# Attention and a gated feed-forward on one core: GpSimd's masks and copies kept from the place right behind a DMA issue, and the order's biases made anew

## The chip, the cores and the metric

One core of one Trainium2 chip runs the whole program. Its engines are TensorE (PE: matmuls and transposes), VectorE (DVE), ScalarE (ACT), GpSimd (POOL) and SyncE (SP, which here only issues transfers). The time is in device microseconds. The kernel before took 303.01 us (median of 3 runs, 302.78 to 303.18).

## The reference

Two layers follow each other. The first is attention over 8 batches, 8 heads, 576 positions and 64 dimensions a head, with a causal mask that lets each query see 32 keys: in the first four heads the last 32 positions, in the other four every fourth of the last 128. The second is a feed-forward from 512 to 2048 and back to 512 over all 4608 tokens, with a gate h * sigmoid(beta * h).

```python
rel = pos[:, None] - pos[None, :]
mask_plain = (rel >= 0) & (rel < 32)
mask_dil = (rel >= 0) & (rel < 128) & (rel % 4 == 0)
attn = softmax(where(mask, q @ k.T / 8, -1e9))          # plain for heads 0..3, dil for 4..7
x = (attn @ v)                                          # (tokens, heads * 64) = (4608, 512)
h = x @ w_in                                            # (4608, 2048)
out = (h / (1 + exp(-beta * h))) @ w_out                # (4608, 512), float32
```

## The kernel before

**Feed-forward.** The 4608 tokens are cut into nine tiles of 512. For each tile and each of 16 blocks of 128 hidden columns, four matmuls (line 887) multiply w_in with the transposed activations `xT` into one bank of PSUM; ScalarE takes a tanh (L896), and VectorE forms the gate `g` (L901). Then 16 matmuls for each 128 tokens (L922, in four parts of four; parts three and four need the second half of w_out) give the output, which ScalarE or VectorE scales (L937, L939) and SP stores (L942).

**Attention.** It is worked batch by batch between the matmuls of the feed-forward. Batches 0 to 2 load q and k directly, and TensorE transposes them (L469, L479); batches 3 to 7 cast them to scratch in memory (GpSimd's queue) and read them back through transposing transfers (L460, on SP's queue). Scores are L652 (tail), L683 (dilated), L711 and L747 (plain); ScalarE takes the exponent (L619); from batch 1 on a mask of zeros and ones is multiplied in afterwards (L623, on VectorE or GpSimd), while batch 0 adds its mask by a matmul (L673, L733, L736). Values are L773 (tail), L788 (dilated) and L804 (plain); VectorE divides by the sum (L638, L639). For batches 0 and 1 TensorE transposes the result into `xT` (L826, L841, L856); later ones go through memory and a transposing transfer (L506 to L533). Copies between tiles (`dkt`, `qt`, `vd`, the halo rows of `vp`) are all on line 243, transfers that GpSimd or SP issues on L394.

**Who sets the order.** All instructions are first recorded as operations with their dependences, a due time `vt`, the engines that may do them, and an expected duration. `Plan.run` then walks a model of the machine forward in time: it keeps when each engine is free, which banks of PSUM are held, how many transfers are in flight on a queue (eight at most), and picks for each engine, of the operations that could start within a few tens of ns of the first (`NEAR`), the one that is due first. So both the order on each engine and the choice of engine come out of it. The order is then fixed in the program: each engine runs its list in order, waiting only for semaphores.

Three details matter for the change:

- Operations that read and write SBUF alone are marked `sbuf` (masks, copies, halo rows, and the making of mask_d and mask_n). Of two such ones on VectorE and GpSimd the model lets only one run at a time (`port`).
- `NUDGE` is a table from an operation's number to a bias in ns, which is added to its possible start when operations are compared. It changes which one is chosen, not any duration.
- Where the model sees TensorE free for more than a bound before the next matmul, in the first 80 us, a filler matmul on zeros is put in (L1035).

GpSimd's copy on L1001 (`pace`) waits until a part of an earlier batch's `xT` (or, for batch 3, of `g`) is there; all loads of a later batch stand behind it.

The comparison in which the change puts its new bound reads, before:

```python
if o.sbuf:
    at = {e: max(t, port["DVE" if e == "POOL" else "POOL"]) for e, t in at.items()}
fin = min(at[e] + d for e, d in o.engs)
```

Of the kernel before, what the change touches and what calls it, by code (L numbers as in the profile page):

```python
# [39 lines left out]
class Plan:  # L40
# [3 lines left out]

    CAPS = {"h": 3, "p": 4, "o": 2, "z": 4, "a": 8, "s": 5, "w": 6}
    SWITCH = 95
    NUDGE = {9: -400, 35: 400, 78: -150, 90: 150, 103: -900, 156: -900, 164: -60, 191: -60, 208: 150,
        220: 900, 247: -400, 251: 60, 266: -150, 268: -150, 270: -150, 326: 900, 376: 400,
        397: 900, 420: 900, 432: -900, 490: 900, 525: 150, 545: 60, 554: 900, 562: -60, 571: 60,
        574: 150, 1103: -400, 1113: 400}  # L50
    LAT = {"PE": 210, "ACT": 45, "DVE": 45, "POOL": 60, "SP": 0}
    NEAR = {"PE": 40, "ACT": 60, "DVE": 60, "POOL": 60, "SP": 0}

# [3 lines left out]
    def op(self, engs, fn, deps=(), vt=0.0, acquire=None, group=None, dma=0, lat=None, halves=False, sbuf=False):  # L57
        acquire = acquire if acquire is None or isinstance(acquire, list) else [acquire]
        o = Op(engs, fn, deps, vt, acquire, group or acquire, dma, lat, halves, sbuf)
        o.bias = self.NUDGE.get(len(self.ops), 0)  # L60
        self.ops.append(o)
        return o

    def run(self, filler=None, filler_until=0.0):
        free = {"PE": 1100.0, "ACT": 1300.0, "DVE": 1000.0, "POOL": 1300.0, "SP": 1300.0}
        dma_free = {"POOL": 0.0, "SP": 0.0, "ACT": 0.0}
        lanes = {"POOL": [], "SP": [], "ACT": []}
        bank_free = {b: 0.0 for b in self.banks}
        held = {}
        for o in self.ops:  # L70
            for d in o.deps:
                d.next.append(o)
            o.waits = len(o.deps)
            o.ready = 0.0
        avail = [o for o in self.ops if not o.waits]
        n_left = len(self.ops)
        n_held = {k: 0 for k in self.CAPS}
        ends = []
        halves = False
        port = {"DVE": 0.0, "POOL": 0.0}  # L80

        def release(now):
            for g in list(ends):
                if g.release <= now:
                    ends.remove(g)
                    n_held[g.kind] -= 1

        def bank_at(gs, start):
            kind, more = gs[0].kind, len(gs)
            n = [x.release for x in ends if x.kind == kind and x.release > start]  # L90
            n_open = sum(1 for x in held.values() if x.kind == kind)
            if n_open + more > self.CAPS[kind]:
                return None
            over = n_open + len(n) - self.CAPS[kind] + more
            if over > 0:
                start = sorted(n)[over - 1]
            open_banks = {x.bank for x in held.values()}
            times = sorted(t for b, t in bank_free.items() if b not in open_banks)
            return max(start, times[more - 1]) if len(times) >= more else None

        while n_left:
            best = None
            near = {}
            for o in avail:
                base = o.ready
                at = {e: max([free[e], base] + [t for x, t in o.group.read.items() if x != e]
                             if o.group is not None and e != "PE" else [free[e], base]) for e, d in o.engs}
                if o.sbuf:
                    at = {e: max(t, port["DVE" if e == "POOL" else "POOL"]) for e, t in at.items()}
                fin = min(at[e] + d for e, d in o.engs)  # L110
                for e, d in o.engs:
                    start = at[e]
                    if start + d > fin + 100:
                        continue
                    if o.dma and len(lanes[e]) >= 8:
                        start = max(start, lanes[e][-8])
                    if o.acquire is not None:
                        start = bank_at(o.acquire, start)
                        if start is None:
                            continue  # L120
                    near.setdefault(e, []).append((start, o, d))
            picks = []
            for e, c in near.items():
                first = min(s + o.bias for s, o, _ in c)
                s, o, d = min((x for x in c if x[0] + x[1].bias <= first + self.NEAR[e]), key=lambda x: (x[1].vt, x[0]))
                picks.append((s, o.vt, e, o, d))
            assert picks, "no work can start"
            s, _, e, o, d = min(picks, key=lambda x: (x[0], x[1]))
            if filler is not None and s <= filler_until and free["PE"] + (300 if free["PE"] < COLD else 170) < s:
                now = free["PE"]  # L130
                open_banks = {x.bank for x in held.values()}
                spare = [b for b, t in bank_free.items() if b not in open_banks and t <= now]
                if spare:
                    filler(max(spare, key=lambda b: -bank_free[b]))
                free["PE"] = now + (225 if now < COLD else 115)
                halves = False
                continue
            for g in o.acquire or ():
                open_banks = {x.bank for x in held.values()}
                g.bank = min((b for b, t in bank_free.items() if b not in open_banks and t <= s + 1e-6),  # L140
                             key=lambda b: -bank_free[b])
                held[id(g)] = g
                g.left = len(g.users)
            o.fn(e)
            if e == "PE" and o.halves != halves:
                halves = o.halves
                d += self.SWITCH
            free[e] = s + d
            if o.sbuf:
                port[e] = s + d  # L150
            o.start, o.end = s, s + d + self.LAT[e]
            if o.group is not None and e != "PE":
                o.group.read[e] = o.end
            if o.dma:
                at = max(dma_free[e], s + d + 900)
                other = max(dma_free.values()) - at
                dma_free[e] = at + o.dma + max(0.0, min(o.dma, other))
                o.end = dma_free[e] + (o.lat or 1100)
                lanes[e].append(o.end)
            avail.remove(o)  # L160
            n_left -= 1
            for x in o.next:
                x.waits -= 1
                x.ready = max(x.ready, o.end)
                if not x.waits:
                    avail.append(x)
            for g in list(held.values()):
                if o in g.users:
                    g.left -= 1
                    if not g.left:  # L170
                        del held[id(g)]
                        g.release = max(u.end for u in g.users)
                        bank_free[g.bank] = g.release
                        ends.append(g)
            ends[:] = [g for g in ends if g.release > s - 5000]
        self.end = max(free.values())
# [892 lines left out]
```

## Time and profile before

| what | us |
|---|---|
| median of the runs | 303.01 |
| profiled execution, its own time | 302.73 |
| its span, first to last instruction | 301.0 |
| PE busy | 295.5 |
| DVE / ACT / POOL busy | 187.5 / 172.2 / 83.9 |
| L922 and L887 matmuls, busy | 140.0 and 137.0 |
| filler matmuls (L1035), busy | 11.6 |
| GpSimd's transfers, share of 16 DMA engines | 59.5% |

Times of instructions are from the start of the span. A line of a timeline gives start, duration, engine, source line, operation, output and inputs, shapes, how many equal ones are merged, and in brackets how long the engine was idle before and what ended that. Matmuls overlap each other, and their ends are modelled: their starts tell more than their durations.

### The profile page before, as it was taken

The numbers are of one execution on the slowest core, as the hardware profiler recorded it, in microseconds if no ns is written. First come the engines' busy times: TensorE is split into PE (matmuls) and PEld (weight loads), VectorE is DVE, ScalarE is ACT, GpSimd is POOL, SyncE is SP. The second block draws the span as 40 slices with busy tenths as digits, with TensorE's granted clock in tenths as the row PEclk, the third lists the DMA queues.
The fourth block names the chain that finished last, engine by engine and source line by source line (L and its number), as shares of the span: only waits on it lengthen the run. The fifth ranks groups of instructions, "written<-read, shape, count | busy, mean of one in ns | idle before, by whom it ended". The sixth has DMA issues, their size and how long they took to land.

```text
span 301.0 us, 6071 instructions
## 1 busy us (share of the span) xinstructions
PE 295.5 (98%) x2344; PEld 150.4 (50%) x2344; DVE 187.5 (62%) x424; ACT 172.2 (57%) x311; POOL 83.9 (28%) x121
## 2 busy tenths in 40 slices
PE   8999999999999999999999999999999999999995
PEld 5866546444554445544444544444454444444454
DVE  4769787798857846887677647865772363343300
ACT  3868764867745744667484548454852654554311
POOL 8997324764236006400730074000000000000000
PEclk9999999999999999999999999999999999999999
DMA  8999999899889998999899979993124100100122
GB/s 164 188 210 201 206 178 222 122 133 145 196 188 197 158 199 173 199 158 191 145 172 158 224 146 173 179 211 90 37 74 117 70 1 35 37 35 35 59 82 70
DMA packets 111248, 41.98 MB, mean 139 GB/s; under 512 B 87620, under 2 KB 104596, under 8 KB 111220
## 3 DMA queue, kind: packets, MB, share of 16 engines
q0 software_dynamic: 60336, 18.58, 59.5%
q1 hardware_dynamic: 50740, 22.95, 37.8%
q8 instruction: 18, 0.29, 0.4%
q14 instruction: 10, 0.08, 0.1%
q10 hardware_dynamic: 144, 0.07, 0.1%
HBM read 37.76 MB, written 18.87 MB: 188 GB/s over the span
## 4 chain that ended last, share of the span: by engine, by line
PE 94%; DVE 2%; ACT 1%; POOL 1%; issue 1%; POOLq 0%; ACTq 0%
PE bank L922 41%; PE bank L887 40%; PE bank L804 2%; PE bank L1035 2%; PE bank L683 1%; PE bank L788 1%; PE bank L711 1%; PE bank L469 1%; PE bank L747 1%; PE bank L479 1%; ACT ptd L619 1%; PE bank L773 1%; DVE xdm L639 1%; PE bank L673 1%; DVE ptd L623 1%
## 5 line engine op out<-in xcount | busy, mean ns | idle before, releaser
L922 PE MATMUL bank<-w_out_bf,g 128*128 128x512 bf16 (+2 forms) x608 | 140.0, 368 | 0.0
L901 DVE SCALAR_TENSOR_TENSOR g<-tnh,bank 128x512 bf16<-128x512 bf16 x144 | 97.3, 685 | 68.2 <-ACT tnh L896 67.2
L896 ACT ACTIVATE tnh<-bank,beta_half 128x512 bf16<-128x512 f32 x144 | 97.9, 690 | 70.3 <-PE bank L887 63.8
L887 PE MATMUL bank<-xT,w_in_bf 128*128 128x512 bf16 (+1 forms) x584 | 137.0, 376 | 0.0
L887 PEld LDWEIGHTS <-w_in_bf 128*128 128x128 bf16 x584 | 55.7, 98 | 62.8 <-issue 0.3
L922 PEld LDWEIGHTS <-g 128*128 128x128 bf16 x608 | 54.5, 98 | 55.7
L937 ACT ACTIVATE osb<-bank 128x512 f32<-128x512 f32 (+1 forms) x35 | 20.6, 589 | 31.3 <-PE bank L922 30.7
L619 ACT ACTIVATE pt<-bank 128x384 bf16<-128x384 f32 (+1 forms) x54 | 20.8, 467 | 6.8 <-PE bank L711 4.3
L619 ACT ACTIVATE ptd<-bank 128x512 bf16<-128x512 f32 x32 | 16.8, 602 | 6.2 <-PE bank L683 6.2
L639 DVE TENSOR_TENSOR xsp<-bank,rcp 96x384 bf16<-96x384 f32 x32 | 17.7, 554 | 1.3 <-DVE rcp L638 0.2
L623 DVE TENSOR_TENSOR pt<-pt,mask_n 128x384 bf16<-128x384 bf16 (+1 forms) x41 | 14.8, 391 | 5.7 <-ACT pt L619 5.5
L638 DVE RECIPROCAL rcp<-bank 128x4 f32<-128x4 f32 (+2 forms) x72 | 12.8, 178 | 5.5 <-PE bank L804 2.4
L1001 POOL COPY pace<-xT 1x2 bf16<-1x2 bf16 x4 | 0.7, 175 | 51.2 <-DMA xT<-x 51.2
L394 POOL DMA_DIRECT2D vp<-in_v_dram x9 | 14.7, 1632 | 0.4 <-PE bank L469 0.4
L623 DVE TENSOR_TENSOR ptd<-ptd,mask_d 128x512 bf16<-128x512 bf16 x27 | 12.0, 465 | 3.6 <-ACT ptd L619 3.0
L639 DVE TENSOR_TENSOR xdm<-bank,rcp 128x256 bf16<-128x256 f32 x32 | 13.6, 425 | 1.1
L394 POOL DMA_DIRECT2D s<-in_q_dram x10 | 13.5, 1351 | 0.0
L394 POOL DMA_DIRECT2D vt<-in_v_dram x16 | 13.3, 993 | 0.0
L1035 PE MATMUL bank<-zero 128*128 128x256 bf16 x67 | 11.6, 310 | 1.3 <-DVE warm L302 1.1
L394 POOL DMA_DIRECT2D s<-in_k_dram x10 | 11.0, 1100 | 1.4 <-issue 1.1
L804 PEld LDWEIGHTS <-pt 128*128 128x128 bf16 x192 | 8.9, 97 | 4.7
L804 PE MATMUL bank<-vp,pt 128*128 128x65 bf16 x192 | 9.8, 193 | 0.0
(112 smaller groups left out, 172.2 us busy)
## 6 DMA issues: line engine op xcount, KB each, us to landing
out_dram<-osb SPq DMA_DIRECT2D x35, 256.0 KB
s<-in_k_dram POOLq DMA_DIRECT2D x10, 288.0 KB, 7.1
s<-in_q_dram POOLq DMA_DIRECT2D x10, 288.0 KB, 10.0
w_out_bf<-in_moe_w_out_dram POOLq DMA_DIRECT2D x2, 1024.0 KB, 16.5
vp<-in_v_dram POOLq DMA_DIRECT2D x7, 288.0 KB, 17.3
st<-in_q_dram POOLq DMA_DIRECT2D x6, 288.0 KB, 11.1
x<-xsp SPq DMA_DIRECT2D x12, 144.0 KB
st<-in_k_dram POOLq DMA_DIRECT2D x5, 288.0 KB, 13.2
```

The source lines that it names most:

```text
L394: {"POOL": nc.gpsimd, "SP": nc.sync}[queue].dma_start(out=out, in_=in_)
L619: nc.scalar.activation(out=w(), in_=sc(), func=ACT.Exp, scale=SCALE)
L623: E[e].tensor_tensor(out=w(), in0=w(), in1=m(), op=ALU.mult)
L638: nc.vector.reciprocal(out=r, in_=p[..., D])
L639: nc.vector.tensor_tensor(out=dst, in0=p[..., 0:D], in1=r.unsqueeze(len(p.shape) - 1).to_broadcast(list(p.shape[:-1]) + [D]), op=ALU.mult)
L804: nc.tensor.matmul(pv[:, a, h2, :], lhsT=lhs, rhs=vp[kv][:, (2 * x + h2) * NI + 3 * j + a, 0:D + 1], start=True, stop=True)
L887: nc.tensor.matmul(bank(g)[:, a:z], lhsT=w_in_bf[:, kt, fb * P:(fb + 1) * P], rhs=xT[:, kt, xo + a:xo + z], start=(i == 0 and kt == kts[0] ...
L896: nc.scalar.activation(out=th[:, 0:n], in_=bank(g)[:, 0:n], func=ACT.Tanh, scale=beta_half[:, fb:fb + 1])
L901: nc.vector.scalar_tensor_tensor(out=g_t[t % 2][:, fb, c0:c0 + n], in0=th[:, 0:n], scalar=1.0, in1=bank(g)[:, 0:n], op0=ALU.add, op1=ALU.mult)
L922: nc.tensor.matmul(bank(g)[:, lo:hi], lhsT=g_t[t % 2][:, fb, tb * P:(tb + 1) * P], rhs=w_out_bf[:, fb, lo:hi], start=(fb == 0), stop=(fb = ...
L937: nc.scalar.mul(out=ob[:, lo:hi], in_=bank(g)[:, lo:hi], mul=0.5)
L1035: nc.tensor.matmul(BANKS[b][:, 0:256], lhsT=zero[:, 0:P], rhs=zero[:], start=True, stop=True)
```

## The change

In the model, an operation marked `sbuf` may not start on GpSimd until 1200 ns after the end of GpSimd's last DMA issue. The table of biases is a new one: 29 entries before and 29 after, of which only one (operation 1113, 400) is in both. Nothing else in the kernel is edited: operations, shapes, transfers and their sizes stay. Since the order and the engine of a great many operations come out of the model, the lists of all engines differ in many places. Source lines behind the edit move by 5: L887 becomes L892, L922 L927, L1035 L1040.

```diff
     CAPS = {"h": 3, "p": 4, "o": 2, "z": 4, "a": 8, "s": 5, "w": 6}
     SWITCH = 95
-    NUDGE = {9: -400, 35: 400, 78: -150, 90: 150, 103: -900, 156: -900, 164: -60, 191: -60, 208: 150,
-        220: 900, 247: -400, 251: 60, 266: -150, 268: -150, 270: -150, 326: 900, 376: 400,
-        397: 900, 420: 900, 432: -900, 490: 900, 525: 150, 545: 60, 554: 900, 562: -60, 571: 60,
-        574: 150, 1103: -400, 1113: 400}
+    NUDGE = {10: 900, 16: -150, 32: -150, 34: 400, 40: -900, 65: -150, 99: -150, 121: -900, 159: -400,
+        165: -400, 190: -150, 215: 400, 222: -400, 362: 900, 382: -900, 422: -900, 426: -150,
+        443: 900, 537: 400, 553: -400, 656: -150, 836: 400, 838: 400, 881: -150, 914: -60,
+        1113: 400, 1133: -900, 1136: 400, 1158: -400}
...
         halves = False
+        issued = 0.0
         port = {"DVE": 0.0, "POOL": 0.0}
...
+                if o.sbuf and "POOL" in at:
+                    at["POOL"] = max(at["POOL"], issued)
                 if o.sbuf:
                     at = {e: max(t, port["DVE" if e == "POOL" else "POOL"]) for e, t in at.items()}
...
             if o.sbuf:
                 port[e] = s + d
+            elif o.dma and e == "POOL":
+                issued = s + d + 1200
```

## The prediction

> **What bounds the kernel now.** I read the page's engine shares first, then the chain that ended last, then TensorE's timeline, looking only for places where a group starts later than the one before it allows.
>
> The busy shares and the chain, from the page:
>
> ```profile
> PE 295.5 (98%) x2344; PEld 150.4 (50%) x2344; DVE 187.5 (62%) x424; ACT 172.2 (57%) x311; POOL 83.9 (28%) x121
> ...
> PE 94%; DVE 2%; ACT 1%; POOL 1%; issue 1%; POOLq 0%; ACTq 0%
> ...
> L1035 PE MATMUL bank<-zero 128*128 128x256 bf16 x67 | 11.6, 310 | 1.3 <-DVE warm L302 1.1
> ```
>
> TensorE is busy for 98% and is 94% of the chain, so an edit to the order can win only what TensorE wastes: fillers (L1035, matmuls on zeros that keep it busy), stalls, and changes of matmul shape. The other engines are far from full. The granted clock is 9 tenths or more in every slice of the page.
>
> TensorE's own timeline shows the waste:
>
> ```profile
> 1.13 3.81 PE L1035 MATMUL bank<-zero 128*128 128x256 bf16 x17 [1.13 <-DVE warm L302]
> 5.13 1.74 PE L673 MATMUL bank<-add_d,ident_b 128*128 128x512 bf16 x4 [0.19 <-POOL add_d L345]
> ...
> 41.43 0.29 PE L788 MATMUL bank<-vd,ptd 128*128 128x65 bf16 x4
> 41.77 0.38 PE L841 MATMUL bank<-ident_b,xdm 128*128 128x128 bf16 x4
> 42.31 0.49 PE L1035 MATMUL bank<-zero 128*128 128x256 bf16 x3 [0.16 <-DVE xdm L639]
> 42.86 0.38 PE L841 MATMUL bank<-ident_b,xdm 128*128 128x128 bf16 x4
> ...
> 62.93 1.02 PE L887 MATMUL bank<-xT,w_in_bf 128*128 128x512 bf16 x4
> 64.69 0.28 PE L788 MATMUL bank<-vd,ptd 128*128 128x65 bf16 x4 [0.73 <-DVE xdm L639]
> ```
>
> Matmuls overlap, so starts count, not durations. Back to back, a 512-column matmul starts every 0.216 us, a 256-column one every 0.109, a 128-column one every 0.056, a 65-column one every 0.029 (starts of neighbours in the trace). Laid end to end at these intervals, all 2344 matmuls of the trace run without a gap except here:
> - start-up, to 30 us: 0.65 us in pieces of about 0.1;
> - 41.4 to 42.9: L841 could start at 41.55, the fillers 0.22 later, the second L841 another 0.33 later; they start 0.22, 0.32 and 0.22 late, 0.75 us in all. They wait for VectorE's normalisation (L639);
> - 64.69: four L887 from 62.93 end at 63.79, so 0.90 is lost;
> - 91.22: 0.20 lost between L922 and L887.
>
> Some 0.8 us more lies in steps too small to name, and from 91 us on no start is over 0.1 late. The stall at 64.69 is the largest; the timeline of all engines shows how it comes about:
>
> ```profile
> 60.04 0.79 DVE L623 TENSOR_TENSOR ptd<-ptd,mask_d 128x512 bf16<-128x512 bf16 x2
> 60.39 2.18 POOL L394 DMA_DIRECT2D s<-in_q_dram  x1
> 61.39 1.55 DVE L623 TENSOR_TENSOR ptd<-ptd,mask_d 128x512 bf16<-128x512 bf16 x1 [0.55 <-ACT ptd L619]
> 61.51 2.42 POOL L623 TENSOR_TENSOR ptd<-ptd,mask_d 128x512 bf16<-128x512 bf16 x1
> 62.86 1.23 DVE L623 TENSOR_TENSOR ptt<-ptt,mask_t 96x256 bf16<-96x256 bf16 x1
> 64.21 0.42 DVE L639 TENSOR_TENSOR xdm<-bank,rcp 128x256 bf16<-128x256 f32 x1
> ```
>
> A GpSimd mask begins while GpSimd's DMA issue (60.39 to 62.57) is still running and takes 2.42 us. VectorE's masks beside it take 1.55 and 1.23 us, where two like the first had just taken 0.79 together. VectorE reaches L639 some 2 us late, and TensorE waits 0.90 of it. This is the pattern that the change names.
>
> **A rule weighed against the row.** The Trainium skill's page "SBUF — State Buffer", section "Who interferes with whom", says that a VectorE instruction with two SBUF inputs contends with a GpSimd instruction that reads SBUF, whichever comes second being blocked. That names the collision of the two masks, not the DMA issue, and so speaks against a change that keeps GpSimd's masks. By it the new order, with eight masks on GpSimd (seven before), would keep the 0.90: the sum below would be -0.8 instead of -1.7. The trace agrees only in part: GpSimd's other masks, away from a DMA issue, take 0.74 us each (mean of five 288-column ones).
>
> **The change part by part**, with the instruction lists of both built programs beside the trace.
>
> 1. *Fillers.* 67 become 65. At the cold start 17 become 18: +0.21 (3.81 / 17 = 0.22 each). Later 50 become 47: 3 x 0.109 = -0.33. Sum -0.1.
> 2. *Shape changes.* Between 64-row matmuls (L479, L683, L711, L747, L826) and full ones the order changes 58 times before, 56 after. Each adds about 0.1: four L922 take 0.86 us in the chain, 0.97 beside such a group. -0.2.
> 3. *The mask at 61.51.* In this stage all four ptd masks now go to VectorE (two, one normalisation, two); GpSimd does copies only. Cost: one more VectorE mask at 0.42, against 1.13 and 0.95 saved on the two stretched ones. TensorE asks for the results with about 0.5 us to spare when I set VectorE's and ScalarE's rows end to end. -0.9, between 0 (the stretch has another cause) and -0.9.
> 4. *The stall at 41.4.* VectorE's four normalisations (0.55 each) had stood too close to L841. Now two g operations and eight L887 lie between, four of the eight pt masks go to GpSimd (4 x 0.74, from about 38.2), and L841 is asked for about 0.5 us after its input. -0.75, between 0 and -0.75.
> 5. *The 0.20 at 91.2* has no releaser that I can name: -0.1, between 0 and -0.2.
> 6. *GpSimd at the start.* ident_f (0.10 and 0.19 us, 0.36 with gaps) moves ahead of ident_b, so add_d ends at 5.45 instead of 5.08. The first L673 slips 0.36, of which part 1's extra cold filler (0.21) is a share: +0.15. mask_t moves behind the weight loads and six input loads; its reader on VectorE is moved to about 18 us and it ends near 16.5, so 0.
> 7. *Loads.* Up to w_out the GpSimd queue keeps its order, and its transfers land one behind the other (w_in's three parts at 15.98, 18.52, 24.03; first w_out at 35.42, second at 42.10), though issued long before. Two w_in issues come 1.1 us earlier, the first w_out issue 1.2 later: no landing moves, 0. But TensorE, now ahead, asks for the w_out halves at about 35.5 and 42.2: +0.1, between 0 and +0.6. For batch 2 the vp load goes behind the others; read at about 68, landing by 54, so 0.
> 8. *Start-up.* VectorE's and ScalarE's evacuations in the new order, set end to end by hand, make TensorE wait 0.3 for the first scores (L683), 0.2 for the second halo copy, 0.2 to 0.3 for transposes: the 0.65 of before in other places. +0.1, between -0.3 and +0.6.
> 9. *SP's queue.* The crossbar of the next batch's q now stands ahead of batch 2's xsp stores. Its cast is issued one place earlier (before, vp took 5.7 us ahead of it: 67.44 to 73.19 landing), so batch 2's transposed x lands no later than the 87.25 of before; first read at about 88.4: 0.
>
> Sum: -0.1 - 0.2 - 0.9 - 0.75 - 0.1 + 0.15 + 0.1 + 0.1 = -1.7 us. The profiled execution took 302.73 (span 301.0 and 1.73 around it): 301.0 after. The runs' median is 303.01, 0.28 above it; so I say **301.3 us**.
>
> **Rivals.**
> - *The order runs nearly as laid out*: 300.3 to 302.2 by the ends of parts 3 to 8. For it: the intervals account for TensorE's whole time but the stalls named, and these are gone from the order as I lay it out. Against it: the walk is by hand over 60 us. 61%.
> - *The rule does nothing on the chip, stalls return elsewhere.* mask_d still stands directly behind a DMA issue in the list, and no wait is added; GpSimd runs it at once. Then only parts 1 and 2 stay, with one or two of the old stalls back: 303.0 - 0.3 = 302.7, to 302.0 with half of parts 3 to 5. 20%, of which 10% within 0.2%, 10% still faster.
> - *Slower: transposed x comes late.* Two pt masks of batch 5 stand on GpSimd behind the next batch's casts, and these behind the copy that waits for batch 4's transposed x (L1006). That landed at 144.10 before; casts take 7.5 us (54.9 to 62.6), so the masks could start at 151.7, and TensorE needs them from about 155. The first L887 of that tile asks at 143.8 or so. From there each us that the landing is later is a us of TensorE, and the slower side begins where 1.7 + 0.6 are eaten, at a landing of 146.1: 147 gives 301.3 + 3.2 = 304.5. Against it: the loop starts about 1 us earlier (the first such copy at 54 rather than 54.78) and in my walk lands near 139. 13%.
> - *Better than laid out*, start-up and w_out cost nothing and drifts of 0.1 vanish: 299.8 to 300.3. 6%.
>
> **Numbers.** 0.2% (0.6 us) is about what a measurement of this kernel tells from no change. Faster: 61 + 10 + 6, 0.77; same 0.10; slower 0.13. Range 300.2 to 302.9: it leaves out the slower case and part of the best one. The likeliest case alone: 300.3 to 302.2.
>
> **What would show it.** After: 65 fillers; no GpSimd mask over 1.3 us; VectorE masks of 512 columns at 0.4 to 0.5 all through 55 to 65 us; no TensorE gap of 0.7 near 64; L841 not late near 42; TensorE's last matmul at 296.0 instead of 297.7. Wrong if TensorE shows gaps over 0.5 us with DMA as releaser at 35, 42, 88 or 144, or if the start-up loses over 1.3 us.

## The result and the profile after

| | before | after |
|---|---|---|
| median of 20 runs, us | 302.92 | 302.35 |
| lowest to highest, us | 302.67 to 304.32 | 301.13 to 303.21 |
| profiled execution, its own time | 302.73 | 302.39 |
| its span | 301.0 | 300.7 |
| PE / DVE / POOL busy | 295.5 / 187.5 / 83.9 | 294.7 / 183.2 / 90.5 |
| TensorE's last matmul starts at | 297.72 | 297.39 |

The ratio of after to before is 0.9974, with a 95% interval from 0.9963 to 0.9986. The kernel got faster, but by 0.57 us by the medians and 0.8 by the ratio, where 1.7 were forecast, and its runs spread over 2.1 us. Source lines of the changed kernel are those of before plus 5.

The engine shares and the chain, from the page of after:

```profile
PE 294.7 (98%) x2342; PEld 150.2 (50%) x2342; DVE 183.2 (61%) x415; ACT 171.3 (57%) x311; POOL 90.5 (30%) x130
...
PE 83%; DMA 9%; POOL 2%; SPq 2%; issue 1%; DVE 1%; ACT 0%; POOLq 0%
PE bank L892 36%; PE bank L927 35%; DMA vp<-in_v_dram 6%; PE bank L1040 2%; DMA xT<-x 2%; PE bank L809 1%; PE bank L793 1%; PE bank L688 1%; SPq L465 1%; DMA x<-xsp 1%; PE bank L716 1%; PE bank L484 1%; PE bank L474 1%; PE bank L752 1%; POOL s L399 1%
```

TensorE is as full as before, yet its share of the chain fell from 94% to 83%. In its place stands one transfer, `vp<-in_v_dram`, with 6% (18 us), and a little GpSimd and SyncE. The chain now leaves TensorE somewhere and goes through the memory loop.

First, the stalls that the prediction named. TensorE's timeline of after, at the places of the old stalls at 41.8 and 64.7:

```profile
40.46 1.89 PE L892 MATMUL bank<-xT,w_in_bf 128*128 128x512 bf16 x8
42.18 0.39 PE L846 MATMUL bank<-ident_b,xdm 128*128 128x128 bf16 x4
42.40 1.03 PE L927 MATMUL bank<-w_out_bf,g 128*128 128x512 bf16 x4
43.27 0.39 PE L846 MATMUL bank<-ident_b,xdm 128*128 128x128 bf16 x4
...
61.49 1.03 PE L892 MATMUL bank<-xT,w_in_bf 128*128 128x512 bf16 x4
62.36 0.28 PE L793 MATMUL bank<-vd,ptd 128*128 128x65 bf16 x4
62.48 0.41 PE L778 MATMUL bank<-vt,ptt 96*128 96x65 bf16 x8
```

Eight 512-column matmuls from 40.46 end at 42.18 (8 x 0.216), where L846 starts; four from 61.49 end at 62.36, where the last dilated value starts. Neither loses anything. VectorE shows why, all four masks at its usual speed:

```profile
57.72 0.75 DVE L628 TENSOR_TENSOR ptd<-ptd,mask_d 128x512 bf16<-128x512 bf16 x2
...
59.42 0.75 DVE L628 TENSOR_TENSOR ptd<-ptd,mask_d 128x512 bf16<-128x512 bf16 x2
...
61.12 0.42 DVE L644 TENSOR_TENSOR xdm<-bank,rcp 128x256 bf16<-128x256 f32 x1
```

Then the new stall. TensorE, VectorE and GpSimd of after, around batch 4's dilated values:

```profile
110.43 0.29 PE L793 MATMUL bank<-vd,ptd 128*128 128x65 bf16 x4
110.56 1.03 PE L927 MATMUL bank<-w_out_bf,g 128*128 128x512 bf16 x4
112.86 0.30 PE L793 MATMUL bank<-vd,ptd 128*128 128x65 bf16 x4 [1.28 <-DVE ptd L628]
...
109.09 0.43 DVE L628 TENSOR_TENSOR ptd<-ptd,mask_d 128x512 bf16<-128x512 bf16 x1 [2.98 <-ACT ptd L624]
111.86 0.48 DVE L248 COPY vp<-vp 32x1280 bf16<-32x1280 bf16 x1 [2.35 <-DMA vp<-in_v_dram]
112.38 1.10 DVE L628 TENSOR_TENSOR ptd<-ptd,mask_d 128x512 bf16<-128x512 bf16 x3
...
87.80 0.18 POOL L1006 COPY pace<-xT 1x2 bf16<-1x2 bf16 x1 [7.50 <-DMA xT<-x]
...
93.65 2.23 POOL L399 DMA_DIRECT2D vp<-in_v_dram  x1
```

Read it from the bottom. GpSimd's `pace` waits 7.50 us for batch 2's transposed x and lets batch 4's loads go; the last is vp, issued at 93.65 and landed at 111.84. VectorE, whose list has the halo copy of this vp ahead of three masks, waits for it with nothing else to do. TensorE could have started its second group at 111.42 (four L927 behind 110.56) and starts at 112.86: 1.44 us late.

The same wait stood in the profile of before, in VectorE's row, without a price:

```profile
111.49 0.48 DVE L243 COPY vp<-vp 32x1280 bf16<-32x1280 bf16 x1 [2.66 <-DMA vp<-in_v_dram]
112.00 1.62 DVE L623 TENSOR_TENSOR ptd<-ptd,mask_d 128x512 bf16<-128x512 bf16 x4
...
113.08 0.29 PE L788 MATMUL bank<-vd,ptd 128*128 128x65 bf16 x4
...
114.06 0.53 PE L788 MATMUL bank<-vd,ptd 128*128 128x65 bf16 x12
```

There vp had landed at 111.46, and TensorE asked for its first dilated value only at 113.08, after the mask: hidden, with about 0.6 us to spare. In after TensorE is there 2.65 us sooner (110.43 for 113.08), of which 0.86 is the order (four feed-forward matmuls fewer lie before it: 352 for 356) and 1.79 is real lead. The landing is 0.38 later, not sooner. In this profile the forecast of 1.7 us was met at 110 us (with a little luck: 0.21 us of the lead is there at the first feed-forward matmul already, where single profiles differ by more); by 113 us most of it was given back. 1.79 less 1.44 is 0.35, and the last matmul is 0.33 earlier.

### The profile page after: what moved, and what is told of

Same layout as the page of the kernel before. It is cut to its first block, busy times and chain, and to the rows that moved or that the text cites. A ratio compares the mean times of both kernels' runs of the same rounds, so it can differ in the third digit from the quotient of the medians.

```text
span 300.7 us, 6078 instructions
## 1 busy us (share of the span) xinstructions
PE 294.7 (98%) x2342; PEld 150.2 (50%) x2342; DVE 183.2 (61%) x415; ACT 171.3 (57%) x311; POOL 90.5 (30%) x130
## 4 chain that ended last, share of the span: by engine, by line
PE 83%; DMA 9%; POOL 2%; SPq 2%; issue 1%; DVE 1%; ACT 0%; POOLq 0%
PE bank L892 36%; PE bank L927 35%; DMA vp<-in_v_dram 6%; PE bank L1040 2%; DMA xT<-x 2%; PE bank L809 1%; PE bank L793 1%; PE bank L688 1%; SPq L465 1%; DMA x<-xsp 1%; PE bank L716 1%; PE bank L484 1%; PE bank L474 1%; PE bank L752 1%; POOL s L399 1%
## 5 line engine op out<-in xcount | busy, mean ns | idle before, releaser
L927 PE MATMUL bank<-w_out_bf,g 128*128 128x512 bf16 (+2 forms) x608 | 140.2, 368 | 0.0
L892 PE MATMUL bank<-xT,w_in_bf 128*128 128x512 bf16 (+1 forms) x584 | 137.6, 376 | 0.0
L892 PEld LDWEIGHTS <-w_in_bf 128*128 128x128 bf16 x584 | 55.4, 98 | 61.5
L927 PEld LDWEIGHTS <-g 128*128 128x128 bf16 x608 | 55.0, 98 | 56.2
L628 DVE TENSOR_TENSOR pt<-pt,mask_n 128x384 bf16<-128x384 bf16 (+1 forms) x39 | 13.0, 349 | 7.0 <-ACT pt L624 6.5
L643 DVE RECIPROCAL rcp<-bank 96x6 f32<-96x6 f32 (+2 forms) x72 | 12.9, 179 | 6.8 <-PE bank L809 3.4
L628 DVE TENSOR_TENSOR ptd<-ptd,mask_d 128x512 bf16<-128x512 bf16 x27 | 11.0, 423 | 5.8 <-ACT ptd L624 5.0
L1040 PE MATMUL bank<-zero 128*128 128x256 bf16 x65 | 11.0, 314 | 1.1 <-DVE warm L307 1.1
L944 DVE TENSOR_SCALAR osb<-bank 128x512 f32<-128x512 f32 (+2 forms) x4 | 2.1, 525 | 14.5 <-PE bank L927 14.5
```

Source lines behind the costliest of these rows:

```text
L628: E[e].tensor_tensor(out=w(), in0=w(), in1=m(), op=ALU.mult)
L643: nc.vector.reciprocal(out=r, in_=p[..., D])
L892: nc.tensor.matmul(bank(g)[:, a:z], lhsT=w_in_bf[:, kt, fb * P:(fb + 1) * P], rhs=xT[:, kt, xo + a:xo + z], start=(i == 0 and kt == kts[0] ...
L927: nc.tensor.matmul(bank(g)[:, lo:hi], lhsT=g_t[t % 2][:, fb, tb * P:(tb + 1) * P], rhs=w_out_bf[:, fb, lo:hi], start=(fb == 0), stop=(fb = ...
L1040: nc.tensor.matmul(BANKS[b][:, 0:256], lhsT=zero[:, 0:P], rhs=zero[:], start=True, stop=True)
```

## Experiments

All times are medians, set beside runs of the kernel before on the same chip (302.77 to 303.15 there).

| kernel | us | lowest to highest | ratio to before, 95% |
|---|---|---|---|
| after, once more | 302.08 | 301.18 to 303.86 | 0.9957 to 0.9992 |
| after, batch 4's halo copy on GpSimd | 302.20 | 301.72 to 302.37 | 0.9965 to 0.9985 |
| before, one mask moved to VectorE | 302.10 | 301.67 to 302.72 | 0.9963 to 0.9986 |
| before, that mask ahead of two issues | 302.38 | one run | |
| the new bound with the old biases | 308.12 | 306.89 to 309.11 | 1.0145 to 1.0191 |
| the new biases without the bound | 305.17 | 304.77 to 306.01 | 1.0058 to 1.0090 |
| after, batch 4's loads released earlier | 301.53 | 301.35 to 302.75 | 0.9943 to 0.9974 |
| before, batch 4's loads released earlier | 302.93 | 302.70 to 303.46 | 0.9986 to 1.0003 |
| after, both edits of batch 4 | 301.72 | 301.52 to 301.84 | 0.9942 to 0.9966 |
| after, loads of batches 4 to 7 released earlier | 303.53 | 301.43 to 307.46 | 0.9973 to 1.0034 |
| after, eight more matmuls at 92 us | 302.30 | 302.20 to 303.14 | 0.9963 to 0.9989 |
| the same with batch 4's loads earlier | 302.35 | 302.11 to 303.03 | 0.9962 to 0.9984 |

### What a GpSimd mask behind an issue costs

The kernel before, with the one mask that stood there given to VectorE:

```diff
-                    E[e].tensor_tensor(out=w(), in0=w(), in1=m(), op=ALU.mult)
+                    E["DVE" if b == 2 and key[0] in (2, 3) else e].tensor_tensor(out=w(), in0=w(), in1=m(), op=ALU.mult)
```

> The kernel before with one instruction moved: the batch-2 ptd mask that GpSimd does at 61.5 us is done by VectorE, at its place in the program. If the stretched masks cause the stall of 0.90 us at 64.7 in full, VectorE's 512-column masks take 0.4 to 0.5 each there, the stall is under 0.1, and TensorE is 0.9 earlier at 70 us. Theory A then has 0.3 of it taken back at 113, where VectorE's wait for batch 4's vp load leaves about 0.65 of room: -0.6 us, 302.3. Without such a wall: -0.9, 302.0. If the stretch has another cause, the stall stays and the time is 302.9.

302.10 us: 0.67 less than before on the same chip. The 0.89 us at 64.69 is gone, the stall at 41.8 stays. Moving one instruction of the old order is worth about as much as the whole change. TensorE and VectorE of that kernel, at the old stall and where a new one opened:

```profile
62.89 1.03 PE L887 MATMUL bank<-xT,w_in_bf 128*128 128x512 bf16 x4
63.76 0.28 PE L788 MATMUL bank<-vd,ptd 128*128 128x65 bf16 x4
...
169.14 0.48 DVE L243 COPY vp<-vp 32x1280 bf16<-32x1280 bf16 x1 [2.02 <-DMA vp<-in_v_dram]
...
170.14 0.29 PE L788 MATMUL bank<-vd,ptd 128*128 128x65 bf16 x4 [0.29 <-DVE ptd L623]
```

The wait that the expectation placed at 113 us did not come there: in this profile vp landed at 110.30, 1.2 us sooner than in before. It came two batches later, at the halo copy of batch 6, where TensorE starts 0.46 us late. By the starts, TensorE is 1.1 us ahead of before at 91 us (the 0.20 at 91.22 is gone here too) and 0.67 at the end: a second kernel that gives a gain back to a load of vp.

The kernel before, with the mask left on GpSimd but the last two of the eight issues (vp and q's cast) put behind it:

```diff
+            lambda e: held_back.append(lambda: dma(queue, *args)) if hold else dma(queue, *args), ...
...
+                    if b == 2 and key[0] in (2, 3) and e == "POOL":
+                        for late in held_back:
+                            late()
```

> The kernel before with GpSimd's last two issues of batch 3's loads (vp, and the cast of q) put behind the batch-2 ptd mask instead of ahead of it, so that the mask runs with the DMA issue done but with VectorE's masks still beside it. If the running DMA issue stretches it: GpSimd's mask takes 1.2 to 1.4 us and VectorE's beside it under 0.6 each. If two masks on the two engines stretch each other: still over 2 us, and VectorE's third mask over 1 us. Time not the question (the two loads start 1.5 to 2.5 us later).

GpSimd and VectorE of that kernel:

```profile
58.27 1.89 POOL L394 DMA_DIRECT2D vt<-in_v_dram  x2
61.40 1.15 POOL L625 TENSOR_TENSOR ptd<-ptd,mask_d 128x512 bf16<-128x512 bf16 x1 [1.24 <-ACT ptd L621]
62.50 1.23 POOL L394 DMA_DIRECT2D vp<-in_v_dram  x1
...
61.77 1.06 DVE L625 TENSOR_TENSOR ptd<-ptd,mask_d 128x512 bf16<-128x512 bf16 x1 [0.55 <-ACT ptd L621]
62.75 0.28 DVE L625 TENSOR_TENSOR ptt<-ptt,mask_t 96x256 bf16<-96x256 bf16 x1
```

Clear of the issue, the mask takes 1.15 us instead of 2.42, the masks on VectorE 1.06 and 0.28 instead of 1.55 and 1.23, and no stall of TensorE remains near 64. So the issue ahead is what made the stall, as the change's name has it (one run, but its rows are plain). A collision of the two masks is left (1.06 where 0.42 is usual, 0.64 us), against the expectation of under 0.6, but it ends in time.

The Trainium skill's page "SBUF — State Buffer", section "Who interferes with whom", has VectorE and GpSimd share a pair of ports under an exclusive lock. The 1.06 us beside a GpSimd mask agrees: VectorE's mask, 0.42 us long alone, ends 0.28 us after GpSimd's. But what the prediction drew from that rule, that the 0.90 would stay, was wrong: what remains of the collision is 0.64 us on VectorE and 0 on TensorE.

### The bound and the biases apart

The new bound with the old table of biases, as a difference against the changed kernel:

```diff
-    NUDGE = {10: 900, 16: -150, ...}
+    NUDGE = {9: -400, 35: 400, ...}
```

> The changed kernel's rule with the biases of before. If the rule itself brings the gain: no GpSimd mask over 1.4 us, and at least 0.9 us less lost before 70 us than in the kernel before, 301.5 to 302.4. If the biases bring it, the rule only reshuffles: 302.7 to 304, with stalls of its own in other places.

308.12 us, 1.7% slower, which neither expectation had, though the second named the reason, a reshuffled order with stalls of its own. GpSimd, VectorE and TensorE of that kernel:

```profile
61.51 2.17 POOL L399 DMA_DIRECT2D s<-in_q_dram  x1
62.62 2.24 POOL L628 TENSOR_TENSOR ptd<-ptd,mask_d 128x512 bf16<-128x512 bf16 x1
...
60.90 1.00 DVE L628 TENSOR_TENSOR ptd<-ptd,mask_d 128x512 bf16<-128x512 bf16 x1
...
127.21 1.67 PE L892 MATMUL bank<-xT,w_in_bf 128*128 128x512 bf16 x7 [2.28 <-DMA xT<-x]
```

The bound did not do what its name says: the mask still begins while the issue runs, and takes 2.24 us. It is a bound in the plan's clock (there the last issue ends at 63.16 and the mask starts at 64.36), not a wait in the program. On the chip GpSimd simply goes on with its list. And the order, reshuffled without its biases, asks for transposed x too early at 127 us: TensorE starts 2.44 us late there, the largest stall of this profile (three near 66 us lose 1.9 more). This is the mechanism that the prediction priced as the slower rival, in another kernel and another batch.

The new biases without the bound:

> The kernel before with the new biases alone, without the bound on GpSimd behind its issues. The order has 86 fillers instead of 67. Theory (biases fit only the model they were made for, as the rule with the old biases showed with 308.1): slower; the fillers alone are 19 x 0.11 to 0.22 = 2.1 to 4.2 us, so 305 to 308. Rival (the biases carry the gain, the bound does little): 301.5 to 302.7.

305.17 us, 0.74% slower, with 86 fillers. Each half of the change alone loses; a table of biases belongs to the one plan it was found for. That the stall at 64.69 went is due to the order they found together, which gives VectorE all four masks there.

### Where the gain went

The changed kernel, with batch 4's halo copy on GpSimd, so that VectorE's masks don't stand behind it:

```diff
-                copy(e, rows[0:WIN, hs, 1:NI, 0:D], rows[QT:P, hs, 0:NI - 1, 0:D])
+                copy("POOL" if b == 4 else e, rows[0:WIN, hs, 1:NI, 0:D], rows[QT:P, hs, 0:NI - 1, 0:D])
```

> The changed kernel with one instruction moved: batch 4's halo copy of vp (L248) goes from VectorE's list to GpSimd's, at the same place in the program; every other list keeps its order. Theory A (the order runs as laid out, and only VectorE's wait for batch 4's vp load gives the gain back): TensorE's gap of 1.3 us at 112.9 goes, and the time falls by 1.0 to 1.4 us against the changed kernel, to 300.9 to 301.4, with a smaller spread between runs. Rival B (batch 3's transposed x, which landed at 116.2 in the changed kernel, stops TensorE anyway): the gap moves to the first L892 of the next token tile near 116.5 and the time falls by less than 0.4 us. Rival C (the loss is not that wait): no gap and no change in time, 302.3.

The stall at 112.86 goes, but the median is 302.20, as far below its neighbour as the changed kernel was (0.57 us): the expected gain is missing, and by the times alone rival C would be right. TensorE meets the next piece of the same lateness:

```profile
108.20 0.59 PE L927 MATMUL bank<-w_out_bf,g 128*128 128x512 bf16 x2
109.09 0.62 PE L688 MATMUL bank<-dq,dk 64*128 64x128 bf16 x16 [0.29 <-DMA dq<-s]
```

It waits for dq, another of batch 4's loads (0.36 us late). In this profile the loads were released at 89.1, 1.3 us later than in after. All seven runs have 2.0 to 2.1 us outside the span, where the other kernels have 1.7 or 1.8 (the new biases alone 1.9 to 2.0); I have no cause for that 0.3. By the span the gain against after is 0.4 us (300.2 for 300.6, medians).

So the start of batch 4's loads was tried itself. `pace` looks at the first half of batch 2's transposed x instead of its middle, which needs both transfers. First for batches 4 to 7 at once:

```diff
-                    xT[0:1, 0, mid - 1:mid + 1] if b - 2 >= BY_DMA else ...
+                    xT[0:1, 0, mid - 2:mid] if b - 2 >= BY_DMA else ...
```

> The changed kernel with the same edit of `pace` for batches 4 to 7. Theory (only batch 4's loads are late; those of 5 to 7 have room, their stalls are 0 in the changed kernel's profile): the same as with batch 4 alone within 0.3 us, 300.8 to 301.5. Rival (once batch 4's wall is gone, the next batch's is the bound): faster than the edit for batch 4 alone by 0.4 us or more. Second rival (loads that start earlier collide with the stores and transposed reads of the batch before): slower by 0.4 us or more.

303.53 us, over a range of 6 us. That is no gain against the kernel before, and 2 us more than with the edit for batch 4 alone, further down: the second rival. GpSimd, SyncE and TensorE of that kernel:

```profile
110.48 0.18 POOL L1006 COPY pace<-xT 1x2 bf16<-1x2 bf16 x1 [7.25 <-DMA xT<-x]
110.96 0.56 POOL L399 DMA_DIRECT2D s<-in_k_dram  x1 [0.30 <-issue]
...
111.57 1.52 SPq L538 DMA_TRANSPOSE xT<-x  x1
...
119.77 1.46 PE L892 MATMUL bank<-xT,w_in_bf 128*128 128x512 bf16 x6 [2.20 <-DMA xT<-x]
```

Batch 4's stall is gone here too (vp landed at 110.48). But batch 5's loads, let go at 110.96 instead of 116.86, now run beside the second half of batch 3's transposed x. It is issued at 111.57 and lands at 119.64: 8.1 us, where after has 3.6. TensorE waits 2.36 us for it. In this profile the pacing of before was what kept that transfer clear.

Then for batch 4 alone, in the changed kernel and in the one before:

```diff
+            look = mid - 1 if b == 4 else mid
...
-                    xT[0:1, 0, mid - 1:mid + 1] if b - 2 >= BY_DMA else ...
+                    xT[0:1, 0, look - 1:look + 1] if b - 2 >= BY_DMA else ...
```

> The changed kernel with one edit: the copy `pace` that holds back batch 4's loads looks at two columns of the first half of batch 2's transposed x instead of two around its middle, so that it waits for the first of the two xT transfers only (84.55 against 87.75 in the changed kernel's profile). All lists stay as they are, the pacing of batches 5 to 7 too. The run with the edit for all four batches had batch 4's vp land at 110.48 and no stall at 112.9, but a new one of 2.36 us at 119.77, where batch 5's loads, let go at 110.8 instead of 116.6, lay beside the transfer of transposed x (8.1 us from issue to landing instead of 3.6). Theory (TensorE, ahead by the stalls it lost, runs into batch 4's loads; their start is the bound): vp lands 1 to 2 us earlier, the 1.44 us at 112.86 goes, none over 0.4 takes its place, 301.0 to 301.7. Rival (any earlier load takes the DMA engines from a transfer that is due sooner): a new stall of over 0.7 us with a transfer as releaser, or a spread between runs as wide as with the edit for all batches (6 us); 302.3 or more.

> The same edit of `pace`, for batch 4 alone, in the kernel before. Theory (before, the wait for batch 4's loads was there too, but hidden by about 0.65 us, since TensorE came later): within 0.3 us of the kernel before. Rival (the DMA loop held back the kernel before as well): faster by 0.6 us or more. Rival (the earlier loads get in the way of others): slower by 0.6 us or more.

The changed kernel gains: 301.53 us, ratio 0.9958, the lowest median here. The kernel before does not: 302.93, 0.08 less than its neighbour. VectorE and TensorE of the changed kernel with this edit, then VectorE of the kernel before with it:

```profile
110.13 0.48 DVE L248 COPY vp<-vp 32x1280 bf16<-32x1280 bf16 x1
110.65 1.10 DVE L628 TENSOR_TENSOR ptd<-ptd,mask_d 128x512 bf16<-128x512 bf16 x3
...
111.02 0.28 PE L793 MATMUL bank<-vd,ptd 128*128 128x65 bf16 x4
111.14 1.03 PE L927 MATMUL bank<-w_out_bf,g 128*128 128x512 bf16 x4
112.01 0.28 PE L793 MATMUL bank<-vd,ptd 128*128 128x65 bf16 x4
...
109.03 0.48 DVE L243 COPY vp<-vp 32x1280 bf16<-32x1280 bf16 x1
111.90 1.89 DVE L623 TENSOR_TENSOR ptd<-ptd,mask_d 128x512 bf16<-128x512 bf16 x4 [2.39 <-ACT ptd L619]
```

The halo copy has no wait in front of it any more (vp landed at 107.28), and TensorE goes on without a gap. In the kernel before the same edit brings vp from 111.46 to 108.02, and that is worth nothing: VectorE's masks now wait for ScalarE, which follows TensorE.

Six runs are few, and the intervals of this kernel and of the changed one overlap. Together with the next kernel, which has the early loads too, there are 11 runs with a median of 301.65; the changed kernel's 32 runs (20 and 12) have 302.27. Eight of the 32 lie between 301.1 and 301.5: the early loads don't beat the changed kernel's best runs, they save it most of the others.

Both edits together, and the changed kernel once more beside them:

> Both edits in the changed kernel: batch 4's loads released by the first half of batch 2's transposed x, and its halo copy of vp on GpSimd. Theory (the halo copy on VectorE and the wait for dq, 0.36 us at 109.09 in the run with the halo copy alone, were the same lateness of batch 4's loads): neither stall, 300.8 to 301.6, the fastest of all, with a spread under 1 us. Rival (as for the edit of `pace` alone): 302.0 or more.

> The changed kernel itself once more, on the same chip as the three edits of batch 4's wait. If the wait for vp is what spreads its runs, its spread stays near 2 us (301.1 to 303.2 before) with a median near 302.35, and the runs with the halo copy on GpSimd spread under 1 us; if the spread came from the chip, all spread alike.

301.72 us over 0.3 us, and 302.08 us over 2.7 us. With both edits the time is in the range that was expected, though not the fastest of all. The spread is as expected too: 0.3 and 0.7 us with the halo copy on GpSimd, 2.1 and 2.7 in the changed kernel. The wait for vp is not all of it, though: with the early loads alone, whose profile has no such wait, six runs spread over 1.4 us. The profiled execution of the repeat happened to be a long one (303.53):

```profile
113.00 0.48 DVE L248 COPY vp<-vp 32x1280 bf16<-32x1280 bf16 x1 [2.84 <-DMA vp<-in_v_dram]
...
114.00 0.30 PE L793 MATMUL bank<-vd,ptd 128*128 128x65 bf16 x4 [1.77 <-DVE ptd L628]
```

vp landed at 112.98 instead of 111.84, 1.14 us later; the execution took 303.53 instead of 302.39, 1.14 us more. Here vp was issued 1.5 us sooner (92.16), but took 20.8 us to land instead of 18.2. Both parts vary: in four profiles with the changed order and the old release, `pace` starts anywhere from 84.4 to 89.1, and vp lands anywhere from 107.5 to 113.0.

Last, the wall from its other side: eight matmuls on zeros in front of one hidden block, work for nothing ahead of the wait, with and without the earlier loads.

```diff
             def mms(e, i=i, kts=kts, a=a, z=z):
+                for _ in range(8 if (t, fb) == (2, 4) else 0):
+                    nc.tensor.matmul(bank(g)[:, 0:256], lhsT=zero[:, 0:P], rhs=zero[:], start=True, stop=True)
```

> The changed kernel with work that means nothing put on TensorE ahead of the wait: eight more matmuls on zeros (256 columns, 8 x 0.109 = 0.87 us) in front of the matmuls of one hidden block near 92 us, behind the issue of batch 4's loads and before the stall at 112.9. Theory (a wall: from 92 us on the time is the later of TensorE's own work and the landing of vp): the stall shrinks by what TensorE is later, most of the 0.87 us vanishes in it, and the median is 302.2 to 302.6, where the changed kernel had 302.08 and 302.35. Rival (the stall is a loss of its own that adds up): 302.95 to 303.2.

> The same eight matmuls on zeros in the kernel whose batch 4 loads are released earlier (301.53 without them). Theory (no wall there): nearly all of the 0.87 us shows, 302.2 to 302.5, and the two kernels with the eight matmuls lie within 0.3 us of each other, where without them 0.55 us or more lay between. Rival (the edit of `pace` saves time in another way than by the wait for vp): 0.5 us or more stays between the two.

302.30 and 302.35 us, as the theory had it: the two kernels, 0.55 us apart in the median without the extra work, are level with it. Where the loads come early, 0.87 us of work cost 0.82. In the changed kernel it cost 0.2 in the median (302.08 to 302.30), while the lowest run rose by 1.0 (301.18 to 302.20): the early runs pay it, and the others, it seems, had that time to wait anyway. No late one was profiled; the profile is of an early one, with no wait for vp. Its loads were released at 84.4, ahead of the eight matmuls and so not by them:

```profile
92.67 1.04 PE L892 MATMUL bank<-zero 128*128 128x256 bf16 x8
...
112.75 0.28 PE L793 MATMUL bank<-vd,ptd 128*128 128x65 bf16 x4
...
110.87 0.48 DVE L248 COPY vp<-vp 32x1280 bf16<-32x1280 bf16 x1
```

## Where the prediction was right and where it failed

1. *Parts 1 and 2, fillers and shapes, -0.3.* 65 fillers and 56 changes, as said. Two fillers fewer are 0.22 us at 0.109 each; what the two changes fewer are worth doesn't stand out of the traces.
2. *Parts 3, 4 and 5, the stalls at 64.69, 41.4 and 91.2, -1.75.* All three are gone in after, 1.84 us. Right, and the cause of the largest is shown: the mask moved alone, and the issues moved alone, each remove it. The 0.20 at 91.22 has no cause still; it is gone in the kernel with the mask moved as well.
3. *Parts 6 and 8, start-up, +0.25.* Not to be seen: the first feed-forward matmul starts at 17.89 to 18.31 us in four profiles with the old order's start and at 17.71 to 18.38 in eight with the new one. *Part 7, w_out, +0.1*: no gap at 35 or 42.
4. *The failed step is what the sum leaves out.* It ends at 91 us, with "from 91 us on no start is over 0.1 late", and takes every microsecond won before as won at the end. Part 9 looked at one transfer behind it, transposed x of batch 2, and found it no later than the 87.25 of before; it landed at 87.75, and between 84.3 and 89.1 in other profiles of that order. That it came no *earlier* while TensorE did was the point. Batch 4's loads hang on it, and the little room behind the halo copy of vp stood in the profile of before. The sum's missing term is a wait at 112.86, +1.44 us: TensorE comes to its second group 2.65 us earlier, and the halo copy is 0.37 later; against that stand 0.34 for the mask that is now done ahead of it, and 1.24 of room that the second group had in before (its mask ended at 112.76, so it could have started at 112.82 and started at 114.06). Taken from the 1.79 us of lead, it leaves the 0.35 that the end shows. The prediction had put every wait behind 91 us at nothing.
5. *The rivals.* "The order runs nearly as laid out" held to 110 us. "The rule does nothing on the chip" is false for the change, but true of the bound by itself, which left the mask behind the issue. "Transposed x comes late" named the right loop, TensorE running into transfers that don't get earlier, but looked at its far end (batch 4's transposed x at 144, landed at 144.36, no stall) and at the slower side only. A wall need not make a kernel slower; it caps what an earlier gain is worth. Two figures of the rivals don't follow from the parts: all the low ends together give 300.7 and all the high ends 304.1, not 300.3 to 302.2, and half of parts 3 to 5 taken from 302.7 gives 301.8, not 302.0.
6. *The signs listed.* Fillers, masks and the two TensorE gaps came out as said; the last matmul did not, at 297.4 instead of 296.0. The signs of being wrong named four places for a gap, none of them 112, and a DMA as releaser, where VectorE stood between the load and TensorE. With batch 4's loads earlier it starts at 296.6, and the time, 301.53, is 0.2 from the forecast.

Not settled: why VectorE's mask took 1.00 us at 60.90 with the old biases, when GpSimd was only issuing (see below); the 0.3 us outside the span; and why one release of the loads comes up to 4.7 us after another.

## What to carry to other kernels

When stalls are taken out of the bounding engine, list behind them every place where any engine waits for a transfer, and its room: the start that needs it, less the landing and what stands between. If the transfer hangs on a loop that the change does not speed up, the gain beyond the room is lost there, and here the runs began to spread with the transfer. A bound in a planner is not a wait: look on the chip whether the instruction moved. And a pacing that looks too tight may guard another transfer; loosen it at one place at a time.

## What the hardware showed that I had not expected

- A GpSimd mask begun during GpSimd's own issue ends about its own length after the issue's record ends: the issue ends at 62.58 and the mask at 63.93 in before (1.35 later), 63.68 and 64.86 with the old biases (1.18); clear of issues the mask takes 1.15. So the stretch looks like a wait that the profile draws as work. The Trainium skill's page "Perfetto Trace Analysis", section "DMA Instruction — SWDGE (GPSIMD)", says that the profile's end of such a transfer is the moment its last descriptor is written; that GpSimd is busy until then would fit the 1.18 and 1.35.
- A VectorE mask can be slow beside issues alone: 1.00 us at 60.90 in the kernel with the old biases, where GpSimd ran nothing but issues until 62.62. In after, VectorE's 27 such masks take 0.427 at most, the four at 57 to 60 us beside issues among them. What makes the difference was not tried.
- The same load of vp, batch 4's, took 17.2 to 20.8 us from issue to landing in 14 profiles.
- TensorE's first matmuls run at half pace up to a moment that differs between executions of one program: the first four 512-column matmuls of the changed kernel start 0.21 us apart in one profile and 0.38, 0.31 and 0.22 in another, though the page's row of the granted clock has 9 tenths from its first slice on in both. This makes single profiles differ by up to 0.6 us at the start, the two that are compared here among them (before 0.38, 0.43 and 0.43). The Trainium skill's page "TensorE: Matmul & The Clock Gate", Part 1, says that the cold stretch varies from run to run; the rows agree.
